# A kernel on one core with its whole instruction order written out: another order, and the last three accumulators copied whole

## The chip, the cores and the metric

The kernel runs on 1 core of one Trainium2 chip. Time is device microseconds (us) of one execution, the median of 3 runs. The engines are TensorE (PE; its weight loads are PEld), VectorE (DVE), ScalarE (ACT), GpSimd (POOL) and SyncE (SP, which issues most DMAs).

## What is computed

A recurrent attention with a complex decay, over 4 batches, 8 heads, 768 steps and head dimension 48; its output is the input of a feed-forward layer with a rational activation (384 -> 2048 -> 384, weights given in 8-byte floats).

```python
def _attn_ref(q, k, v, a_re, a_im):
    mag = np.sqrt(a_re * a_re + a_im * a_im)
    scale = np.minimum(mag, 0.999) / (mag + 1e-06)
    a_re_n, a_im_n = (a_re * scale, a_im * scale)
    ...
    for t in range(S):
        new_re = ar * S_re - ai * S_im
        new_im = ar * S_im + ai * S_re
        kv = np.einsum('bhd,bhe->bhde', k[:, :, t], v[:, :, t])
        S_re, S_im = (new_re + kv, new_im)
        y[:, :, t] = np.einsum('bhd,bhde->bhe', q[:, :, t], S_re)

def _moe_ref(x, w_in, w_out, a, b):
    h = x @ w_in
    h2 = h * h
    h3 = h2 * h
    P = a[0] + a[1] * h + a[2] * h2 + a[3] * h3
    Q = 1.0 + np.abs(b[0]) * np.abs(h) + np.abs(b[1]) * h2
    g = P / (Q + 1e-06)
    return (g @ w_out).astype(np.float32)
```

## The kernel before

The sequence is cut into 6 chunks of 128 steps; a chunk of one batch is a *unit*, so there are 24 units, taken in 12 pairs. For each unit the code records these steps:

- `norm` loads the decays (AA), squares and roots them, and makes the running product of their sizes MM (scans on DVE, three a unit) and the angle T. A small copy keeps the last column of MM in `ncar` for the next chunk.
- `angle` (once a pair) sums the angles, reduces them to one turn and makes the argument of the cosine, CO; `trig` takes arctangents, sines and cosines on ACT, which needs another activation table than the roots do.
- `outer` (line 569) loads QK and V, makes the factors RU out of MM, multiplies QK by RU, multiplies the result by CO and by T (two tiles Q) and has six DMAs copy the Q tiles into HQ, where a head's 96 rows lie on partitions.
- `attn` (line 599) transposes (PE, line 611), makes scores (line 624) with a mask ST, values (line 642) and the states for the next chunk (line 662), and writes the result into X, in two parts: rounded, and what is left.

The weights come in 8-byte floats: `weights` and `fold` (line 416) load 28 blocks (384 or 512 KB) into few staging buffers (`g` four, `wh0` to `wh2` one each) and put each block together in four steps, the last two on DVE (lines 443 to 449). `split` and `halve` (line 461) part them into a rounded and a left-over half. A buffer is loaded anew only when its block is done, so SP waits there.

The feed-forward `ffn` (line 678) runs eight times: twice on the first pair and second pair with whole fp32 weights, twice more on a pair each, then four times on two pairs with 512 columns. Each has 16 blocks: `first` (line 701) makes ph, ten or so operations of ACT, DVE and POOL (helpers at lines 351 and 366) make g, `reduce` (line 717) adds into the accumulators po. At its end po is scaled and copied (`evac`, line 380), and stored.

Nothing runs in the order in which it is recorded. `Plan` collects 2600 operations with what they read and write, and with the engines that each may run on; `recorded` (line 185) unpacks the string ORDER into a sequence of operation numbers, each with one of its allowed engines, checks that each stands behind all that it depends on, and the kernel emits them in that sequence. Each engine works its own operations off strictly in this order, and so do the queues of SP and of ACT, which also issues a few DMAs. An operation that waits holds up all behind it on its engine. `rouse` (line 667) records dummy matmuls, each of which may run on PE, or as nothing at all on SP: the order decides which. A product of two tiles in SBUF mostly may go to DVE or to POOL, a copy of kT or po to ACT or DVE, a weight step to two or three engines.

In the last feed-forward (`end`) each of the three accumulators po (512 columns) is copied in two halves, the first on ACT, the second on DVE, and stored by one DMA; that of the last one is issued by ACT.

Of the kernel before, what the change touches and what calls it, by code (L numbers as in the profile page):

```python
# [232 lines left out]


ORDER = (
    "c-lo+33yaR*1gq9x|2Xs6+jR&kO1Ni!=Q{fjsu8*D2OcMf`UP1SGJ%KWF0nvfb0VTf&x11_~U?pqJWBujx(dkfI^x@L`J9zOBO=+nNzQW|CjIe>wd55)~$Qb"
# [3 lines left out]
    "xW?Gfe`CcMEjQAOwT#bRyO5qm=!=T3l;6riEXS*%A9dsSPxdfcOJnmdn<BT#T1GXd{uPU(nzWQAW`R|*2Kn+cZVw%d`8@f*R}toCvcz<<%aoxFrX5werA11z"  # L240
    "a+ND)<d;fF_Tz@obU!1PvFFMuGLLa9kW~U)iVv4bXrNAH)^dsWD%Td>AY+M(kuFW{#SU8VE1ikgR!YKhJ~N|O$;J3oJ}cxkMh~;oq?sJTbg4>P5xEa_B#mP)"
    "W=`OKUzJDdzkO^y{=-;&jhjux%!rP|Khag5lnQ!30l+^PgZZ>IMF#3AwuV}v+v(}iJ@~hza`jT&i%qCWixrrGF?{w@J>?d<4X7>;nPk_CvEE5P71viBUxq@Q"
    "B=QREYVNgjPVVur6zY*KUC!V|J(u@abg3OhYgKqfI3txPPsFn~YRZhjQW=I~sr18H+%5;{`)XN@okZIh943-?Vt2ijQ6<Y|U;G0`Wil<L%AXjuKiSJzB6HA7"
    "R%s>Axl6?A2l0<(0%J3Umg5+UjrF7Gd~9R=?Xh;pmmp;Nx<Z^lk}Q-usz-dfjKWm$e$7QZ=TK1-&iV!qU@t4TuXyw%nRB)Y>trhZtiW@)L-OQhaD07LG#2~x"
    "9yb>QWU<aGt|P<a*U4GpZzSIXh4ghCF2Km7`h$;UnlWw^Hpo%j!1Z3xvt2&o7%b1o3VM@euA<l`oBDFh4#pw_46x)2`Ku|lRRlUks>svK@OnHg)0wxK(x2bI"
    ")s5Xl^nISL=`QFoc9cnxnl4G25KCt{`)}wb#~8!jSjk`C>e+UZ8SD-d0}(09JR>7q8LqNMx9E<}=V3Y8bI0f8CfW@1D(AbuqIZD$mvnaVFjSz22}!!k(GR#C"
    "dLn0ij8t>LUd46NtFlfyasTDmrH{y4tfO&yl6ze<uI>m<lG{$oOI-a5*=`{#IhEP{9=DSHK9ZS?!w51+4Aaa``!MUZg|6c6;h2}@3*2Q6;1TQNdPHt!6clSs"
    "$xQh>=8#i%>h><*OtpS}M_ehfD4^XK2FY&S!BvrII79qL$XrSW$p`%Wf>kt#JNyHYyN{JogLs+Bd?>lBBQB1%L_ux5OOHm&C5$oIv>wAmxz+S@{qPEkq#YUh"
    "0_#P|6S4)HiISGsCbyE4ydTwh^)<J+;rNAKl%N^My~t;!y!R)<l}yD;(lobO^ffFq1ME!x>MHlhIvry5t|F?Z$ZmAi<+2z>wxN^+R*%P(tY#FF$SbRvqmOVS"
    "pN_yBS)}{9+On5+KS6i-fxA|+3oG!p9KnRjn!8K7NCA3CQ~8t~C{;??2@cuDe3S3rn_;d3qmeDc$k8F$hBq1M#*!^b%mRq&&a@ViiTV|{iOh3`QR^u~^%z&3"  # L250
    "y8_CHbw#8+=$gs~c87ZOyepBr2zh+|XL(a^u)Cxy9+&s^9Ji6N&*xs75IOtMKIoU__zZVTy1d5yJ<LvbFINWkBC6NhJo>PLzON0ewd792%=HSS%V)YfpS0zE"
    "d+P06J4N2ZCFZj=;}?>5g8WRx5Shn3?9xZ=R*oKuq+mzN_`14XI`a1mtjy-}C9W})XT-DY#tr$c3tl8@Q{`^+5jNTW;;Xn5-ZlG)iYb`Pk&kl5JjuW_M#&p|"
    "njtFSx-9vQPcy{#?vd=v+st!zo$k$5YkGz;9b7JFe~jC>8_y0t54X4>{PcLvXAIxPA=(+n91mcXe$W215jQb1hxBOo6;A3#?2AdJhC74WoV^dehku7}CEYBw"
    "Q{l6Fk=e<TyXATI&k*-9US7vi6tRn!>)Q0B1pmP-lkRS3J~v@E{R)%qhA>La$RZDOMvg2)M_PJ^aoS-9;#SV;Cqs0hTga}t9vfvVa~)<y{lLz?nI4?yl`Grz"
    "Z=LUI>vWQ9z<ln(ol;ApdaHd_x|_jvKJ~!!_I_!>N>=h1?T5(iJJ>H2eN2{a^0aB^P9lfv#-s=F_Z(EvMY<7l?{m#v>{QP)mx~ZHL#*FR7UNlnU9_-+RdgEr"
    "(Od?ip&nJ-mrs}BGJLNb&Yl)xWJ1zjd}Y6dCmGY~?EFfeG4pM8uDyl(|Cl&^f{N&LkW0UIvJ|mDrStnAseqIW;oIf#8SiM;;4bdB8b_W(6FG=G`R->#;cLk2"
    "E6Y78Q_F$#_rUkix`CEc%wJ)ktt#*(t+yvL`lsXFDc+BxKe23NdcYk^ut!=^Rh*{PQ`9kgIJ%sbKy?;ix+UM;DF0*(LuBJ}oYHk!ufSa5RGGH!J)*7^*Zc!n"
    "t!i-_Uj+eD_ewo>lrQ=1G?LWCco#B9$kdbLI$Bi9s(YP2KSq@L9_c$}9acwGMsS<yWPz=$&9|AQwz5N>_BG2oc*rIyDMdW$vSpT}QxATDf8%;p4R@H@ZaZ3t"
    "S4vl~n%H}X{&hwjM&~T6<uYE!vqXFhUY(}V#uQZ17hJPI&9vscrOY__)TFsp`h*)pw#<;<Im#ERh#}P8laLhTc9?9ULQt+kKk5c!HnW?bsD7DFJy&Q;u!b{E"
# [853 lines left out]
```

## Time and profile before

| | us |
|---|---|
| median of 3 runs (607.23 to 609.35) | 608.46 |
| the profiled execution | 608.84 |
| its span, from first to last instruction | 607.1 |
| PE busy in the span | 558.8 (92%) |
| DVE busy | 545.7 (90%) |
| ACT busy, table loads included | 527.1 (87%) |
| POOL busy | 275.4 (45%) |

Over the whole span the DMA engines moved 64.02 MB; the first quarter carries most of it. Matmuls of one group overlap in the records, so a busy PE is not PE at its peak. A row of a timeline gives start and duration in us, engine, line, operation, what it writes and reads, how many instructions it merges and, in brackets, how long the engine stood idle before it and what ended that.

### The profile page before, as it was taken

Reading aid. Unit: us, or ns where it says so; the run is one execution under the profiler, and the core shown is the slowest. Engines: PE = TensorE matmul, PEld = TensorE weight load, DVE = VectorE, ACT = ScalarE, POOL = GpSimd, SP = SyncE. Lnnn points to the kernel's source line nnn. Section 1 sums busy time; section 2 is a strip of 40 time slices with the busy share of each in tenths; the row PEclk is TensorE's granted clock in tenths of the full one; section 3 lists DMA queues with packets and bytes.
Section 4 is the critical chain, followed back from the end, with each engine's and each line's share of the span. In section 5 each row is a group of like instructions: output and inputs, shape, how many; then the busy total and the mean of one; then the engine's idle time right before and its main releaser. Section 6 shows DMA issues by size and latency. Waiting matters only on the chain.

```text
span 607.1 us, 15647 instructions
## 1 busy us (share of the span) xinstructions
PE 558.8 (92%) x6236; PEld 468.3 (77%) x6236; DVE 545.7 (90%) x918; ACT 527.1 (87%) x870; POOL 275.4 (45%) x264
## 2 busy tenths in 40 slices
PE   3258989999999999998999999999999999999995
PEld 2246878778899999996888877888888888778884
DVE  6989979989999999999999999988899978779983
ACT  6978989989999999999999989988978787587871
POOL 4456455255655556624684544464726066200000
PEclk9669999999999999999999999999999999999998
DMA  8899436436551455537227147233464235010001
GB/s 268 282 253 285 148 79 152 111 57 149 110 136 41 89 128 127 129 103 154 51 64 157 35 106 168 74 60 82 75 102 127 26 73 103 3 52 2 1 1 58
DMA packets 39185, 64.02 MB, mean 105 GB/s; under 512 B 4416, under 2 KB 25152, under 8 KB 39104
## 3 DMA queue, kind: packets, MB, share of 16 engines
q1 hardware_dynamic: 38960, 62.67, 42.2%
q8 instruction: 51, 0.84, 0.6%
q14 instruction: 30, 0.25, 0.1%
q10 hardware_dynamic: 144, 0.26, 0.1%
HBM read 39.32 MB, written 4.72 MB: 73 GB/s over the span
## 4 chain that ended last, share of the span: by engine, by line
PE 47%; DVE 5%; ACT 3%; issue 1%; DMA 1%; DVEq 0%; ACTq 0%
PE po L717 20%; PE ph L701 20%; PE at L642 3%; PE at L624 2%; ACT Zf L366 1%; DVE Af L351 1%; PE at L662 1%; DVE Q L351 1%; DVE ph L351 1%; DMA AA<-in_aa 1%; PE at L611 1%; ACT Af L366 1%; DVE ST L351 0%; DVE g L351 0%; DVE MM L351 0%
## 5 line engine op out<-in xcount | busy, mean ns | idle before, releaser
L717 PE MATMUL po<-g,wh 128*128 128x512 f32 (+1 forms) x576 | 167.6, 360 | 0.0
L701 PE MATMUL ph<-X,wiH 128*128 128x512 f32 (+1 forms) x576 | 144.3, 363 | 2.2 <-DVE Af L351 2.2
L717 PE MATMUL po<-g,wo 128*128 128x256 f32 (+1 forms) x462 | 141.8, 370 | 0.1
L717 PEld LDWEIGHTS po<-g,wh 128*128 128x128 f32 x576 | 102.8, 189 | 18.2 <-issue 1.4
L701 PEld LDWEIGHTS ph<-X,wiH 128*128 128x128 f32 x576 | 97.3, 188 | 20.1 <-issue 1.4
L717 PEld LDWEIGHTS po<-g,wo 128*128 128x128 f32 x462 | 87.3, 191 | 12.5 <-DVE g L351 0.5
L351 POOL TENSOR_TENSOR g<-Af,Zf 128x512 fp32r<-128x512 f32 x30 | 40.2, 1341 | 115.7 <-ACT Zf L366 59.9
L351 DVE SCALAR_TENSOR_TENSOR ph<-Zf,co,ph 128x512 f32<-128x512 f32 x96 | 71.8, 748 | 8.9 <-ACT Zf L366 5.9
L366 ACT ACTIVATE Zf<-ph,co 128x512 f32<-128x512 f32 x96 | 65.3, 680 | 10.4 <-PE ph L701 5.6
L351 DVE SCALAR_TENSOR_TENSOR g<-ph,co,Zf 128x512 fp32r<-128x512 f32 x80 | 59.6, 745 | 14.7 <-ACT Zf L366 13.6
L366 ACT ACTIVATE Zf<-Af,co 128x512 f32<-128x512 f32 x80 | 57.8, 723 | 16.3 <-DVE ph L351 13.9
L366 ACT ACTIVATE Af<-Af,co 128x512 f32<-128x512 f32 x96 | 68.7, 720 | 0.8
L701 PE MATMUL ph<-X,wi 128*128 128x512 f32 (+1 forms) x264 | 67.4, 359 | 0.0
L351 DVE SCALAR_TENSOR_TENSOR Af<-Af,co,g 128x512 f32<-128x512 f32 x80 | 65.1, 814 | 2.2
L366 ACT ACTIVATE Af<-ph 128x512 f32<-128x512 f32 x96 | 56.2, 589 | 8.8 <-PE ph L701 8.6
L351 DVE SCALAR_TENSOR_TENSOR Af<-ph,co,Af 128x512 f32<-128x512 f32 x80 | 59.7, 746 | 1.4
L701 PEld LDWEIGHTS ph<-X,wi 128*128 128x128 f32 x264 | 45.7, 188 | 8.1
L366 ACT ACTIVATE Zf<-Zf 128x512 f32<-128x512 f32 x80 | 50.4, 630 | 1.8
L701 PE MATMUL ph<-wh,wi 128*128 128x256 f32 x192 | 45.9, 387 | 0.9 <-DVE g L351 0.9
L701 PEld LDWEIGHTS ph<-wh,wi 128*128 128x128 f32 x192 | 35.6, 190 | 7.1 <-issue 1.6
L351 POOL TENSOR_TENSOR SQ<-SQ 128x384 f32<-128x384 f32 x18 | 21.8, 1212 | 35.9 <-ACT SQ L366 35.8
L624 PEld LDWEIGHTS at<-HQ 96*32 96x32 f32 x1536 | 30.6, 113 | 9.7 <-ACT kT L357 3.7
(203 smaller groups left out, 1088.7 us busy)
## 6 DMA issues: line engine op xcount, KB each, us to landing
HQ<-Q SPq DMA_DIRECT2D x144, 128.0 KB, 5.0
AA<-in_aa SPq DMA_DIRECT2D x23, 384.0 KB, 4.1
QK<-in_qk SPq DMA_DIRECT2D x23, 384.0 KB, 4.2
V<-in_v SPq DMA_DIRECT2D x24, 320.0 KB, 5.3
wh<-in_w_in SPq DMA_DIRECT2D x6, 512.0 KB, 6.2
g<-in_w_out SPq DMA_DIRECT2D x8, 384.0 KB, 5.6
wh<-in_w_out SPq DMA_DIRECT2D x8, 384.0 KB, 6.4
g<-in_w_in SPq DMA_DIRECT2D x6, 512.0 KB, 6.6
```

The source lines that it names most:

```text
L351: call = lambda e: getattr(e, kind)(*map(real, args), **{k: real(x) for k, x in kw.items()})
L366: e.activation(o(), i(), f, **kw)
L611: e.transpose(pt[:, i].bitcast(F32R), hq[:, 4 * g + i, 1, :], ident)
L624: e.matmul(pst[32 * q:32 * q + 32, i + y, s0:C], hf[:, h, 1, s0:s0 + 32], hf[:, h, 0, s0:C], start=True, stop=True)
L642: e.matmul(py[32 * y:32 * y + 32, min(j, 2), :], l, sts[h // 4][:, h % 4, :] if q is None else hf[:, h, 0, :], start=q is None and j == 0, ...
L662: e.matmul(pd[m:m + 32, h], kT[:, h, m:m + 32], V[:, n:n + D], start=True, stop=True)
L701: e.matmul(o, wt[f // 4 * NJ + j][:, f % 4 * P:f % 4 * P + P], moving(j, hl), start=n == 0, stop=n == len(prods) - 1)
L717: e.matmul(o[:, cols], wt[:, j * P:j * P + P], gg, start=(f == 0 and n == 0 and cols.start == 0), stop=(f == NFF - 1 and n == len(prods) - ...
```

## The change

The string ORDER is replaced. As the new string unpacks, it holds 2597 operations: 863 on DVE (857 before), 792 on ACT (787), 235 on POOL (246), 420 on PE (418; 31 dummy matmuls instead of 29), 287 on SP (292). 179 of the operations that both orders have change their engine, and most change their place by some tens of operations, within the same course of units and feed-forwards. Six copies of accumulator halves become three copies of whole accumulators: in the new order DVE copies the last one, ACT the middle one, then DVE the first one.

```diff
 ORDER = (
-    "c-lo+33yaR*1gq9x|2Xs6+jR&kO1Ni!=Q{fjsu8*D2OcMf`UP1SGJ%KWF0nvfb0VTf&x11_~U?pqJWBujx(dkfI^x@L`J9zOBO=+nNzQW|CjIe>wd55)~$Qb"
...
+    "c-lQ!2Y8m%6@I@zJ0!U`EE#PQz)_{e5vUZEB?z(vg$gR5EKvhNnIXsq6Gen1j0izMhKwo%P-#I?P*jMvMW_`*0%5cW`EJ4pS^w#KZ>Z1z{Nww+JI;B}d){;I"
...
 )
@@ ffn @@
         for o, _, n, j in cuts:
             ob = buf(ff, [P, 512], F32, *(("Zf", ZB) if j == 0 else ("Af", AB) if F == 2 or j == 1 else ("wo15", 1)))
-            for h in range(2) if end else (0,):
-                m = n // (2 if end else 1)
-                cols = slice(h * m, h * m + m)
-                evac(m, lambda ob=ob, cols=cols: ob[:, cols], lambda o=o, cols=cols: o[:, cols], (o, "co"), ((ob, h),),
-                     minus if whole else sc, ("ACT", "DVE")[h:h + 1] if end else None)
+            evac(n, lambda ob=ob, n=n: ob[:, 0:n], lambda o=o, n=n: o[:, 0:n], (o, "co"), (ob,), minus if whole else sc)
```

## Rows read from the trace of the kernel before

**Rows 1.** Windows: stretch, length, busy us per engine, PEclk, DMA share, GB/s
```profile
0.00:60.00 60.00, 30.21 (x317) 23.32 (x318) 49.87 (x108) 48.22 (x90) 29.70 (x47) 0.80 0.91 274
60.00:100.00 40.00, 37.29 (x267) 30.83 (x265) 36.12 (x61) 36.50 (x61) 23.12 (x28) 0.96 0.48 122
100.00:360.00 260.00, 252.38 (x3526) 221.61 (x3526) 248.55 (x415) 245.21 (x404) 138.67 (x125) 1.00 0.45 103
360.00:600.00 240.00, 238.89 (x2131) 192.52 (x2129) 210.30 (x335) 196.38 (x316) 83.87 (x65) 1.00 0.29 62
90.00:100.00 10.00, 9.85 (x97) 7.75 (x95) 9.59 (x18) 9.00 (x17) 6.69 (x8) 0.83 0.60 135
```

**Rows 2.** The page, busy time of each engine over the span
```profile
PE 558.8 (92%) x6236; PEld 468.3 (77%) x6236; DVE 545.7 (90%) x918; ACT 527.1 (87%) x870; POOL 275.4 (45%) x264
```

**Rows 3.** Timeline, 0 to 61 us, single rows of DVE, ACT, POOL and PE
```profile
5.51 0.16 DVE L391 RECIPROCAL co<-ab 128x1 f32<-128x1 f32 x1 [1.85 <-DMA ab<-in_coef]
...
23.57 0.83 ACT L565 ACTIVATE T<-T 128x768 f32<-128x768 f32 x1
...
27.24 0.93 DVE L351 TENSOR_TENSOR Q<-QK,CO 128x768 f32<-128x768 f32 x1
...
38.59 0.57 DVE L443 SCALAR_TENSOR_TENSOR po<-po,wh 128x384 uint32<-128x384 uint32 x1 [2.89 <-ACT wh L439]
...
41.35 0.19 POOL L351 COPY ncar<-MM 128x3 f32<-128x3 f32 x1 [4.24 <-DVE MM L351]
...
50.41 0.86 PE L611 MATMUL at<-ident,HQ 128*128 128x128 f32 x8 [1.92 <-DMA HQ<-Q]
...
55.42 0.91 PE L701 MATMUL ph<-wh,wi 128*128 128x256 f32 x3
...
60.49 0.75 DVE L351 SCALAR_TENSOR_TENSOR ph<-Zf,co,ph 128x512 f32<-128x512 f32 x1
```

**Rows 4.** Groups by form: count, then busy us and mean ns, then idle before
```profile
L351 POOL TENSOR_TENSOR QK<-QK,RU 128x768 f32<-128x768 f32 x12 | 24.2, 2014 | 8.6 <-DVE RU L351 4.4 <-DMA HQ<-Q 3.4 <-DMA QK<-in_qk 0.4
L351 DVE TENSOR_TENSOR QK<-QK,RU 128x768 f32<-128x768 f32 x11 | 10.4, 949 | 1.8 <-DMA QK<-in_qk 1.8
L351 POOL TENSOR_TENSOR Z<-MM,Z 128x384 f32<-128x384 f32 x17 | 22.3, 1311 | 33.0 <-ACT Z L366 33.0
L351 DVE TENSOR_SCALAR Zf<-po,co 128x512 f32<-128x512 f32 x2 | 1.5, 751 | 0.3 <-PE po L717 0.3
```

**Rows 5.** Waits of SP's queue, 0 to 60 us: total us, times, longest
```profile
SPq L345 <- DVE wi L447: 12.7, 5, 5.6
```

**Rows 6.** Timeline, 79 to 96 us, single rows of SP, POOL and DVE
```profile
79.09 1.21 SPq L345 DMA_DIRECT2D HQ<-Q  x2
80.39 0.55 SPq L345 DMA_DIRECT2D QK<-in_qk  x1
...
87.61 1.80 POOL L351 TENSOR_TENSOR QK<-QK,RU 128x768 f32<-128x768 f32 x1 [3.40 <-DMA HQ<-Q]
...
90.41 0.56 DVE L351 SCALAR_TENSOR_TENSOR SQ<-AA,SQ 128x384 f32<-128x384 f32 x1 [3.29 <-POOL T L351]
...
92.96 0.95 DVE L351 TENSOR_TENSOR Q<-QK,T 128x768 f32<-128x768 f32 x1
...
93.19 2.46 POOL L351 TENSOR_TENSOR Z<-MM,Z 128x384 f32<-128x384 f32 x1 [2.81 <-ACT Z L366]
```

**Rows 7.** Timeline, 598 to 602 us, copies and the last store
```profile
598.78 0.47 ACT L357 ACTIVATE Zf<-po,co 128x256 f32<-128x256 f32 x1 [4.50 <-PE po L717]
...
599.29 0.48 DVE L351 TENSOR_SCALAR Zf<-po,co 128x256 f32<-128x256 f32 x1 [1.92 <-ACT Zf L357]
...
600.08 0.47 ACT L357 ACTIVATE wo<-po,co 128x256 f32<-128x256 f32 x1 [0.82 <-PE po L717]
...
601.49 0.33 SPq L345 DMA_DIRECT2D out<-Af  x1
```

**Rows 8.** Waits of PE for a DMA of HQ, whole span: total us, times, longest
```profile
PE at L611 <- DMA HQ<-Q: 4.7, 3, 2.0
```

More of the change, by code (lines that the diff above doesn't have):

```diff
@@ L240 @@
[L240 to L259, printed above, removed]
@@ new lines @@
+    "9|DiBYVi=}ens+KCJ~52D;$?7RPjkr?tzz7S>&Na0=lK~P?>nX=$bS~Ip1?IQM{zLi#<KjUyKZ?7KJl%kh4P2R|?QbT49<VV3HGe6rYfnxaK8EL}-#%9Eq_Q"
+    "$KPkUM@t;md;N^WGesVscsQlc`E4bDTDdA4^jrQW{9Rt)+!g46aKs}{M7E(VLXo7(%tdJ~ouJ@zrLV9{vgKLqmf`4)p0Y=K=0g>2Jl&h`J+f4J#g}Mt<KnCQ"
+    "+*;h19!JRy&WuKy&hR~2m78d7*o%*x_iJS&)+AbcqcD=ATObhw-Srr(N-QmU72U8~g<-RQT~6yI{wmH|ulM;OSSP>8bQskKy?swN)Ypiim$Z#*--kCO9Fue#"
+    "|1w8M;T41+PZqQcIsLuV!=pIXqOdSAFt2tSt=}o}E;bF&q~(c14*{&;oKQw=e#@T=o3#uU<<|Z;acprzER_oSlvjM1Yut;Gk`h=^8->OAPCmtd;+mGtm5GU-"
@@ new lines @@
+    "DfOGtipxa0yeJyYJYl3x2JiIBgC6Zj!WfB2$}OIYS>oxFeuZp8X)qh(xu?b`yyt8Q(B6USc5-1JVo@olgE8=QG_8#&s|rSYU8RH0Gy%t-8j)Z<FI9z`w>fgM"
+    "WFu30NgHpXq$tnS!!Wca4?aMIUhR*^yAq)z%nlV^7R8xiXe}p@Dxr+|e)%J#aYXv*Q1dDlsS-bnc4WyZ`3L#7m|l2zk?+!kgfk_<t+Z#HsUZ?oGG3-jQ!hh;"
+    "GKHvxVXX3yYrap|T|65F!TY>wGA)L-1)Oi8?sKTL)HCSc2%_Mb7Uc9+T$d4K_bPtdk;D0<Aimq_`h3<2tz<b8b(ERT$a<KM3Yj4b5P^C`E)z32V-fFlz%cSM"
+    "8Y|UFW=npsyXWDHglXn+V^^Gy6>6A?!GmP`&IGUc5Sn3~{??DgWNEHT`~><R&bNor9GxO-ouzMz;hnS6M~-1T21$u%Wb*#K`k#J|6v-PzDc5>|B0nfu%=T##"
@@ new lines @@
+    "jcf9j%lT?73tpym4RxOQwBj3NFxv6Dl4EM*Wx4LRK(Q>=P4HhoONyCwHR>6EGpbaC8IIK|O)W1@l~f&yMgBy6k113sX1N+?w#oza{+}{R#vw)r<u#L~ZZi=$"
+    "ubP<tI4!p$;4-fo8|69v-bOB5mPY!V^kkm?&eV!krAS64pBnHyHZTiU$qSsb9Ix=nbjiRb&J_8Us7{vua72OXVBWx)xLh+LX;e`%^W-(`<GNea5YrB;B~rKH"
+    "Zl{s&hce#NsaS=<+daF>Ec{kd$mzdIJ3g6-rgA5Brajhhr$fk>R2-7eBnErrgiOW9@*v*hh>!8O6iQPZK!2i~%*glDANn=KIGkR8t9qIFl7=N@?+Cm@_1eRy"
+    ")G)b%NNKBQ=&y>>AS%~yt-tVzzT7|)nZbCr!sECpE6C^<Y1=2#i&tODzZj({NWmicSUqJ@sTb?zOMEJS=gK=}J|o(LSFO;I<7RP2J&e-(%{cLc0djgQtio;M"
@@ new lines @@
+    "vxC@&<IMF3a8*5ImeH#h@U0$N>R}>U>j^}^y!0qF=tmhAH>xb4|Lxlx&PJXZZN8G_9B&b$CdvjX&H-LmOK-Gi1Rf@WB6C!sZ+TfO8?iu*GC?^m_hJhX@$heI"
+    "*>)L(9NK)G^M}&k1@b<#;&Iy8kR!TaxLR-iCEL|3vsZqLbJAV^<bR+-%}l&)by^27gFHQ^R+<j7lm6^*`55W;-YIt9r?}1r8Nkm^WFQW6_XhlIPcChcpH!yV"
+    "E{CW9XU!U7G>|&iidlM$kuO#8CIssluYuIMD^&hu-Olu8rnkf!da&P5D^o?($DkJiT70L1-0_AC<6bYxYK&2NCKi|F8zOR@PY!U`^)jA2AC$K-LAo#}j9TwU"
+    "vx@vAqwzV%RY*T-)n2Z)R3>npKTAHxUn8<z$i=7BZhG5Ct;NpZ=&}X2!pUV?dzH9f;Z-B%PMOmqYCk&aC;STHkj|X2+4l=}1atJ=)UhqnM*rwvlUQ8DpTt(@"
@@ new lines @@
+    "8fk<gx!@G~A@pJ-I-x+?;tMsMtZ0KDXiW(#$|rIj-Q{ko;Blfi*&GaZ^a5Zs^#b2kqN(^<Yy?`;l4V5wudbSQBZB4BkW-BQ@9_vTz7_B6lBRkIt$CU{5<x|J"
+    "(?4$`s9xrdsYquA1yD%*{~@)Kj5}DxAH!MI7|M)63&zpIX6Es2!Qp}Bao0_}!`Q=ko$cSGwyzSSV!67)FYbOrBJ`trn5=z(wiU>IP6^{#5kA*@SgltQ1^a42"
+    "-|nV$vFJg47{S=S;^*ki%*hZu%@~OD$i5ax3vZ<Ry^4CVoLX=vaZ15mRO7CAN{{z%kl6t;;&Up4Ma0wd%nx#tJQ#uynS<B4=Fd37T6RRNg<p%c^$A+hN&bcp"
+    "qyeq##XPOgxua><PppA^IHE5Zvr+ECAN6`h(Z;(6Ge&dNhmxkx`bBb>QFs<M11?E_KHn=Z;i}7wJeL(cIMyepzHkw50L!F4+V}_L8PrE6qaLBpQyGKo>cZ&r"
@@ L276 @@
+    "|5XT9)xH?`l%3Btvfv~m;1SsdE;H?!K9;E8v};m}?0+exQs;HFV`(Mhc!5>CPRqhwrM35M{PwaZ=9Q~a;Z9@f7-l`MWqw)q=v)5@R60NE5Dh_Ht+Ux$>6D~C"
+    "_pqyk5RXuYu-y93As!Y#+ojdsTHE#WJa5?OMYxfbWKfiirBgBMbp<;IYfH6=s@pZ}*EJ(yTy1;A|Bhpt{_1btu2oJg>voFZuWH9yPlua2EwkrtJKEO$m|O7)"
+    "zvY)jlPbYZAWR3zo>~=VYUF=QQFeI"
 )
```

35 lines of the change are left out of this document (16 added, 19 removed).

## The prediction

> **What bounds the kernel now.** I read the windows view first, in four stretches [rows 1]. From 0 to 60 us TensorE computes for 30.2 us only: the 16 DMA engines are 0.91 busy and VectorE 49.9 of 60 us. From 60 to 100 us TensorE works 37.3 of 40 us; from 100 to 360 us it works 252.4 of 260, with VectorE at 248.6 and ScalarE at 245.2, so three engines are nearly full at once; from 360 to 600 us TensorE works 238.9 of 240 us and sets the pace alone. The 7.1 us that are left to the span's end hold the last copies and stores. The page's line of busy time [rows 2] gives the same over the span: TensorE 92%, VectorE 90%, ScalarE 87%, GpSimd 45%.
>
> So no order can give much. What can be won is idle time of VectorE before about 360 us: from 0 to 60 us 10.1 us, of which 5.5 us come before its first work on loaded data [rows 3], so 4.6 us; from 60 to 100 us 3.9 us; from 100 to 360 us 11.4 us [rows 1]. After 360 us only an earlier start helps.
>
> **The change part by part.** I decoded both order strings against the kernel's recorded list and summed, for each engine, the mean durations of the rows grouped by form ([rows 4] has four of them) over all work queued ahead of one operation ("work ahead" below; rows overlap a little, so the sums stand some 7% above busy time).
>
> *What stays.* The order is valid as written: each operation comes once and behind what it depends on. The trips between trigonometric and root tables are 23 in both, so table loads don't change. Of 2591 common operations 179 change their engine; the total lists change by -3.4 us on VectorE, +1.9 us on ScalarE, +7.1 us on GpSimd. VectorE's list ahead of its first operation of the first feed-forward (at 60.49 us [rows 3]) is 53.2 us before and 52.8 after; ahead of the first feed-forward's fifth g 80.3 and 80.3; ahead of the first g of the sixth feed-forward 370.8 and 367.4. Bytes queued ahead of the last HQ copy of the first unit are 8.88 MB in both, of the second unit 11.88 MB in both. The gains have to come from waits inside the lists.
>
> *Front, to 60 us.* VectorE's longest wait there is 2.89 us at 38.59, for a weight block whose transfer came late [rows 3]. In the new order that step has 38.8 us of work ahead, not 30.4, so the blocks that are already there go first: the wait goes, and what is late next is the queue itself. GpSimd's 4.24 us wait at 41.35 [rows 3] goes too: it is a 3-column copy that stands ahead of the second unit's last Q product and waits for a scan with 32.7 us of VectorE work ahead; in the new order that scan has 24.0. So Q is whole some 4 us earlier, and its six DMAs, two of which ScalarE now issues, are no longer late against TensorE's 1.92 us wait at 50.41 [rows 3]. SP's queue is moved too: it waits 12.7 us for VectorE's weight folding [rows 5]; in the new order nine transfers go out before its first wait, not seven. Against this stands one new wait: the first unit's product with the sines goes from GpSimd to VectorE, and ScalarE gets four more operations, 2.6 us, ahead of the sine that starts at 23.57 [rows 3]. If ScalarE has no idle time it starts by 24.2, otherwise at 26.2, and ends 0.83 later; VectorE reaches the product with 20.6 us of work ahead, and before the change it was 21.0 us into its list at 27.24 [rows 3], so it arrives about 26.7: a wait between 0 and 0.4, and I take 0.4. Sum: 2.9 - 0.4 = 2.5 us, between 0 (the DMA engines decide) and 4.6 (all idle time goes).
>
> *60 to 100 us.* VectorE waits 3.29 us at 90.41 for GpSimd's T, which stands behind a product that waited 3.40 us for the fourth unit's QK transfer [rows 6]. SP issues that at 80.39, 1.30 us after the first HQ copy of the unit before, behind two copies [rows 6]; now one copy stands ahead, which saves 0.6 us. The third unit's product, 0.95 us on VectorE, goes to GpSimd at 2.01 [rows 4], as does one more Q product, which leaves VectorE 1.9 us lighter there. I take 1.0 us of 3.3, ends 0 and 3.3. The clock fell here once, to 0.83 in the mean of 90 to 100 us [rows 1], between its levels of 2.4 and 1.2 GHz, after TensorE had been waiting; 3.4 us at the lower level cost at most 1.7 us, counted only for the range.
>
> *100 to 360 us.* VectorE's list is 3.4 us lighter by the sixth feed-forward, but ScalarE is as full as VectorE [rows 1] and its list there is only 2.1 us lighter. I take 1.2 us, ends -3.4 and +3.4: the trace can't show which waits a new order makes, and their likeliest size is that of the ones they replace.
>
> *Dummy matmuls.* 31 run instead of 29, in time when TensorE waits: nothing; if that cover is gone, under 1 us.
>
> *Tail.* Three accumulators were each copied half by ScalarE, half by VectorE, and the halves ran one behind the other (598.78, then 599.29; the VectorE half waited for ScalarE's) [rows 7]. Now VectorE copies the last accumulator whole, then the first; ScalarE copies the middle one. A whole copy takes 0.75 us on VectorE [rows 4]. The last matmul released the last accumulator's copy at 600.08 [rows 7]; two copies behind each other end at 600.08 + 0.75 + 0.75 = 601.58, and SP issues the last store then, against 601.49 [rows 7]: 0.1 us lost, ends -0.5 and +0.7.
>
> Sum: 2.5 + 1.0 + 1.2 - 0.1 = 4.6 us. From the span of 607.1 us that leaves 602.5; 1.74 us lie around the span (608.84), and that execution stands 0.38 above the median 608.46: 603.9 us.
>
> **The rivals.**
> - *Transfers set the front, and nothing is carried on.* For: the DMA engines are 0.91 busy up to 60 us [rows 1], with equal bytes ahead of both units, equal lists on VectorE. Against: VectorE and SP stand waiting for each other there [rows 3, 5]. Then the front gives 0, the middle up to 1, the tail -0.1: 607.1 + 0.1 + 1.36 = 608.6 down to 607.6, no difference; I put it at 607.9.
> - *Longer chains on GpSimd (slower).* The product QK of a unit is on GpSimd in 17 units instead of 12, at 2.01 us instead of 0.95 [rows 4], and it stands in the chain product, Q, HQ copy, transposes and scores. Five units, 1.06 us each, are 5.3 us, if in each the HQ copy is what TensorE waits for last; it decides from the point where the copy lands later than the feed-forward work queued beside it runs out. Against: GpSimd is 45% busy [rows 2], and TensorE waited for that copy 3 times, 4.7 us in all [rows 8]. With the front's 2.5 gained and no more: 607.1 + 5.3 - 2.5 + 1.74 - 0.38 = 611.3.
> - *VectorE loses to GpSimd what it hands over.* A GpSimd multiply of 384 columns took 2.46 us at 93.19, beside two VectorE products of 0.95 each, against 1.31 in the mean [rows 4, 6]. So far GpSimd pays, not VectorE. If VectorE paid for the 7.1 us that GpSimd's list grows, half of it would take back 3.6 of the 4.6 us: 607.5. The Trainium skill ("SBUF — State Buffer", Who interferes with whom) says that a VectorE instruction with two SBUF inputs contends with a GpSimd instruction that reads SBUF, and that the later one to issue blocks whole. By that rule VectorE would pay wherever GpSimd issues first; the trace shows GpSimd paying.
> - *The string is not taken* and the kernel plans its own order: its length and its dependencies fit, so 0.01.
>
> **How the numbers follow.** Forecast 0.50 (own range 599.5 to 606.4), front bound by transfers 0.22, GpSimd chains 0.20, VectorE pays 0.05, others 0.03. All the terms at their upper ends and the clock come to 4.6 + 2.1 + 2.3 + 2.2 + 0.6 + 1.7 = 13.5 us; they will hardly meet, so the lower end takes some 6 us beyond the forecast: 598.0. The upper end takes in the slower rival: 611.4. A measurement of this kernel can tell about 0.3%, 1.8 us, from no change: faster 0.52, same 0.25, slower 0.23.
>
> **What would show it.** Right: no VectorE wait near 38 us, the first feed-forward's matmuls before 53.5 us instead of 55.42 and VectorE's first operation on them near 58 instead of 60.49; the wait for T under 90 us short of 2.5 us; the last store issued 1.5 us behind the start of the last accumulator's copy. Wrong: TensorE's first transposes of the second unit not before 50 us (transfers), or waits of TensorE for HQ copies in units whose product moved to GpSimd (slower).

## The result

The changed kernel takes 601.15 us (median of 4 runs, 599.88 to 602.38), the kernel before 608.9 beside it (607.23 to 610.21): ratio 0.9874, 95% interval 0.9838 to 0.9911. It is faster by 1.3%, 7.7 us; the forecast was 603.9 us, 4.6 us below the median then known. Its profiled execution took 602.15 us, with a span of 600.5; that of before had 607.1.

The windows of the changed kernel (as [rows 1]):

```profile
0.00:60.00 60.00, 29.27 (x306) 22.74 (x307) 50.12 (x107) 46.89 (x88) 31.04 (x46) 0.77 0.87 266
60.00:100.00 40.00, 40.00 (x364) 34.76 (x363) 38.92 (x74) 39.72 (x69) 24.13 (x25) 1.00 0.58 140
100.00:360.00 260.00, 256.36 (x3475) 225.65 (x3474) 249.05 (x418) 246.04 (x408) 149.29 (x127) 1.00 0.46 106
360.00:600.00 240.00, 232.68 (x2101) 187.03 (x2099) 205.57 (x328) 192.09 (x311) 79.86 (x56) 0.99 0.26 62
90.00:100.00 10.00, 10.00 (x177) 8.53 (x176) 10.00 (x21) 9.94 (x19) 6.98 (x9) 1.00 0.71 139
```

Read TensorE first, the first figure with a count. From 60 to 100 us it worked 37.29 us and now works all 40.00; from 100 to 360 us it worked 252.38 and now 256.36 [rows 1]. Its idle time in these two stretches fell from 10.33 to 3.64 us, by 6.7 us, and the span fell by 6.6. These figures count dummy matmuls as work: in the first feed-forward eleven of them run now and eight before, and where ten are moved away (below) 3.45 us of idle time come back there and that stretch gets no longer. Up to 60 us TensorE works less than before, at a lower clock. The page's line of busy time has hardly moved [rows 2], since the work is the same:

```profile
PE 558.3 (93%) x6240; PEld 470.2 (78%) x6240; DVE 543.7 (91%) x924; ACT 524.7 (87%) x872; POOL 284.3 (47%) x253
```

The front, single rows of the timeline (as [rows 3]):

```profile
24.61 0.96 DVE L351 TENSOR_TENSOR Q<-QK,CO 128x768 f32<-128x768 f32 x1 [0.41 <-ACT Q L357]
...
48.34 1.23 PE L611 MATMUL at<-ident,HQ 128*128 128x128 f32 x8 [4.43 <-DMA g<-in_w_out]
...
51.91 0.69 DVE L351 TENSOR_TENSOR ST<-at,cmask 128x512 f32<-128x512 f32 x1 [4.70 <-ACT ph L431]
...
56.70 2.75 PE L701 MATMUL ph<-wh,wi 128*128 128x256 f32 x12
...
61.05 0.75 DVE L351 SCALAR_TENSOR_TENSOR ph<-Zf,co,ph 128x512 f32<-128x512 f32 x1
```

VectorE's wait of 2.89 us at 38.59 and GpSimd's of 4.24 at 41.35 [rows 3] are gone, and the one new wait that I priced at 0.4 us is there with 0.41. But the first feed-forward's matmuls start at 56.70 us, not before 53.5 as I wrote; before it was 55.42. The second unit's transposes come 2.07 us earlier (48.34 against 50.41 [rows 3]), and from there to the first feed-forward 8.36 us pass instead of 5.01. The windows say why (stretch, length, TensorE's busy time, granted clock, DMA share, GB/s; 0.50 is the level of 1.2 GHz, 1.00 that of 2.4):

```profile
44.00:46.00 2.00, 0.00 (x0) 1.00 1.02 223
46.00:48.00 2.00, 0.00 (x0) 0.59 1.03 369
48.00:50.00 2.00, 1.66 (x10) 0.50 1.01 372
54.00:56.00 2.00, 2.00 (x33) 0.50 0.00 0
56.00:58.00 2.00, 2.00 (x8) 0.85 0.36 48
```

TensorE had come to the upper level shortly before (0.76 in the mean of 42 to 44 us) and then stood idle from 43.9 to 48.3 us; the level fell, and the whole second unit was computed at half speed. Before the change TensorE was at 1.00 in each 2 us from 48 to 56, though it had stood idle there too, for 1.92 us [rows 3].

From 60 to 100 us, rows of GpSimd, SP and VectorE (as [rows 6]):

```profile
75.98 1.81 POOL L351 TENSOR_TENSOR Q<-QK,T 128x768 f32<-128x768 f32 x1
...
77.82 0.33 SPq L345 DMA_DIRECT2D QK<-in_qk  x1
78.20 3.17 SPq L345 DMA_DIRECT2D HQ<-Q  x5
...
84.21 1.82 POOL L351 TENSOR_TENSOR QK<-QK,RU 128x768 f32<-128x768 f32 x1
...
87.44 0.55 DVE L351 SCALAR_TENSOR_TENSOR SQ<-AA,SQ 128x384 f32<-128x384 f32 x1
```

The fourth unit's QK load goes out at 77.82, not 80.39; GpSimd's product does not wait (3.40 us before), VectorE's step behind T does not wait (3.29 us before [rows 6]). The label of the 3.40 us names an HQ copy, but it was the QK load: that landed at 87.47 us, and the product started at 87.61. The tail (as [rows 7]):

```profile
592.52 0.69 ACT L357 ACTIVATE Af<-po,co 128x512 f32<-128x512 f32 x1 [4.87 <-PE po L717]
...
593.20 0.75 DVE L351 TENSOR_SCALAR wo<-po,co 128x512 f32<-128x512 f32 x1 [2.40 <-PE po L717]
...
593.86 0.74 DVE L351 TENSOR_SCALAR Zf<-po,co 128x512 f32<-128x512 f32 x1
...
594.63 0.33 SPq L345 DMA_DIRECT2D out<-Zf  x1
```

The last store is issued 1.43 us behind the start of the last accumulator's copy, against 1.41 before [rows 7].

### The profile page after: what moved, and what is told of

It is laid out like the page before. It is cut to its first block, busy times and chain, and to the rows that moved or that the text cites. A ratio compares the mean times of both kernels' runs of the same rounds, so it can differ in the third digit from the quotient of the medians.

```text
span 600.5 us, 15652 instructions
## 1 busy us (share of the span) xinstructions
PE 558.3 (93%) x6240; PEld 470.2 (78%) x6240; DVE 543.7 (91%) x924; ACT 524.7 (87%) x872; POOL 284.3 (47%) x253
## 4 chain that ended last, share of the span: by engine, by line
PE 46%; ACT 11%; DVE 8%; issue 2%; DMA 1%; SPq 0%; DVEq 0%; ACTq 0%
PE ph L701 20%; PE po L717 19%; ACT Zf L366 4%; PE at L642 4%; PE at L624 2%; DVE Af L351 2%; ACT Af L366 2%; DVE g L351 2%; DVE ph L351 2%; PE at L662 1%; ACT L366 1%; ACT SQ L366 1%; DMA QK<-in_qk 1%; DVE Q L351 1%; PE at L611 1%
## 5 line engine op out<-in xcount | busy, mean ns | idle before, releaser
L717 PE MATMUL po<-g,wo 128*128 128x256 f32 (+1 forms) x462 | 140.3, 367 | 0.0
L351 POOL TENSOR_TENSOR RU<-MM,RU 128x384 f32<-128x384 f32 x18 | 22.7, 1259 | 39.4 <-DVE RU L351 33.4
L351 DVE TENSOR_TENSOR ST<-at,cmask 128x512 f32<-128x512 f32 x48 | 31.6, 683 | 10.1 <-ACT ph L431 4.7
```

The source lines that it names most:

```text
L351: call = lambda e: getattr(e, kind)(*map(real, args), **{k: real(x) for k, x in kw.items()})
L717: e.matmul(o[:, cols], wt[:, j * P:j * P + P], gg, start=(f == 0 and n == 0 and cols.start == 0), stop=(f == NFF - 1 and n == len(prods) - ...
```

## The experiments

In the table, "ratio" is against the kernel before on the same chip, with its 95% interval. The other columns come from the one profiled execution of each kernel: the start of the first feed-forward's first matmul; from there to the end of its last (A); from there to the end of the last matmul of the fifth feed-forward (B); from there to that of the eighth (C). Span less these is the tail, 6.9 to 7.6 us in all of them.

| kernel | ratio | first matmul, us | A | B | C |
|---|---|---|---|---|---|
| before | 1 | 55.42 | 58.95 | 252.07 | 233.61 |
| changed | 0.9874 (0.9838 to 0.9911) | 56.70 | 53.57 | 249.15 | 233.74 |
| changed, again | 0.9880 (0.9844 to 0.9917) | 52.49 | 54.65 | 248.59 | 233.74 |
| new front, old rest | 1.0019 (0.9998 to 1.0040) | 53.65 | 59.49 | 249.58 | 234.29 |
| old front, new rest | 0.9914 (0.9881 to 0.9946) | 54.04 | 54.75 | 248.38 | 233.72 |
| new to 103 us, old rest | 1.0008 (0.9978 to 1.0038) | 56.15 | 59.96 | 250.66 | 234.00 |
| new to 219 us, old rest | 0.9913 (0.9886 to 0.9940) | 54.22 | 53.67 | 250.28 | 234.27 |
| old to 220 us, new rest | 0.9981 (0.9953 to 1.0009) | 55.14 | 58.30 | 249.83 | 233.74 |
| before, own QK buffer | 0.9977 (0.9948 to 1.0006) | 55.23 | 55.89 | 251.32 | 233.87 |
| before, early third unit | 0.9938 (0.9907 to 0.9968) | 54.31 | 57.41 | 252.76 | 233.57 |
| changed, late QK load | 0.9882 (0.9848 to 0.9916) | 54.23 | 54.94 | 249.04 | 234.58 |
| changed, QK on VectorE | 0.9837 (0.9803 to 0.9871) | 52.94 | 54.44 | 252.35 | 232.74 |
| changed, dummies moved | 0.9861 (0.9825 to 0.9898) | 52.70 | 53.65 | 248.60 | 233.74 |
| and waits filled | 0.9832 (0.9804 to 0.9859) | 53.23 | 53.41 | 249.08 | 233.72 |

Executions of one kernel differ: 26 of the kernel before on one chip lie between 604.38 and 611.95 us. The first column shows where much of that comes from: 52.49 and 56.70 us in two executions of the same changed kernel, whose spans differ by 3.8 us. A and B repeat better, so I read stages from them and whole times from the ratios.

### Which stretch gains: two pairs of exchanged orders

My theory, from the two traces: the new front gives nothing, all gain is made behind it. The rival is my prediction: the front gives 2.5 us. An order is a list; a first part of one and, of the other, all that is not in it make a valid order. Here and below, most fences with + and - tell in words which part of an order, or which steps of an engine's queue, moved.

```diff
# new front, old rest: against the order of before
-old[0:263]
+new[0:244]
 old, what is left
# old front, new rest: against the changed order
-new[0:244]
+old[0:263]
 new, what is left
```

> The new order up to the first matmul of the first feed-forward (its first 244 operations), then the old order for all that is left; the last accumulators copied whole. My theory, read from the two traces: the new front gives nothing (first feed-forward matmul at 56.70 us against 55.42 before), because TensorE runs at the lower clock level from 46.5 to 57 us; all of the gain is made behind it. Then this kernel takes what the old one takes, 608 to 610 us, and VectorE's wait of about 3 us for T near 90 us is still there. Rival: the new front is worth 2.5 us as I predicted, and the first feed-forward's late start is made up by work done ahead: 605.5 to 606.5 us.

> The reverse of the run before it: the old order up to the first matmul of the first feed-forward (its first 263 operations), then the new order for all that is left; the last accumulators copied whole. My theory (the new front costs 1.3 us and the rest gains): first feed-forward matmul at 55.4 us, whole time 599 to 602 us, as good as the changed kernel or up to 1.3 us better. Rival (the front's 2.5 us are real and are carried on): 603 to 604.5 us, some 2.5 us worse than the changed kernel.

Measured: 609.44 us for the new front with the old rest, 602.74 for the old front with the new rest, the kernel before 608.0 beside them. The first matches my theory: the front alone brings nothing. Three rows show what it ran into:

```profile
79.09 0.54 SPq L345 DMA_DIRECT2D QK<-in_qk  x1
...
87.90 0.50 PE L611 MATMUL at<-ident,HQ 128*128 128x128 f32 x4 [2.01 <-DMA HQ<-Q]
...
89.18 0.56 DVE L351 SCALAR_TENSOR_TENSOR SQ<-AA,SQ 128x384 f32<-128x384 f32 x1 [3.37 <-POOL T L351]
```

Both waits of the old order are there in full. A is 59.49 us although the clock is at 1.00 all through 60 to 100 us in this trace: the waits alone cost the time, the fall of the clock to 0.83 [rows 1] is no condition for it. The old order up to 220 us (below) does not show that fall either, and its A is 58.30. The second, 5.3 us faster, lies just above my theory's 599 to 602 and just below the rival's 603 to 604.5: with the new rest behind it, the front may be worth up to some 2 us, and the intervals of 0.9914 and of the changed kernel overlap.

The same with later seams:

```diff
# new to 103 us
+new[0:500]
 old, what is left
# new to 219 us
+new[0:1082]
 old, what is left
# old to 220 us
+old[0:1088]
 new, what is left
```

> The new order for its first 500 operations (to about 103 us, the third unit's and the fourth unit's products with it), then the old order for all that is left; the last accumulators copied whole. The trace of the changed kernel is 4.7 us ahead at the end of the first feed-forward's last first-layer matmul, 2.5 us ahead at 270 us and 7.0 us ahead at 366 us. My theory (two separate gains, the first made between 60 and 100 us and kept, the second made behind 100 us by the new order there): 603 to 605 us. Rival A (the first gain decides everything, and the rest of the old order simply runs on from it): 600.5 to 602.5 us. Rival B (the first gain is given back in the old order's waits): 606 to 608 us.

Measured: 609.18 us, no gain. The waits of its TensorE from 88 to 125 us (total us, times, longest):

```profile
PE at L623 <- ACT kT L356: 4.7, 1, 4.7
```

The lead of the first feed-forward was lost in this one wait at 105.7 us, at the seam, where operations that the old order had done earlier piled up on GpSimd; ScalarE, which copies kT, waited 3.14 us for GpSimd's MM. Behind the wait the clock fell once more, to 0.83 in the mean of 110 to 120 us. The run says nothing of the old order behind it. So the next seams lie where the two lists have done nearly the same.

> The new order for its first 1082 operations (to about 219 us, a place where the two orders have done nearly the same), then the old order for all that is left; the last accumulators copied whole. The run with the seam at 103 us lost its lead in one TensorE wait of 4.7 us at the seam, so it told nothing of the stretch behind. My theory (two gains: about 4.7 us made by 220 us, and about 2 us more made behind it, in the stretch from 270 to 366 us): this kernel keeps the first alone: 602.5 to 605 us, profiled span near 602. Rival (the order behind 220 us does not matter, the old one has the same waits): as good as the changed kernel, 600 to 602 us. Rival (the lead is given back in the old order's later waits): 606 to 608 us.

> The reverse: the old order up to about 220 us (its first 1088 operations), then the new order for all that is left; the last accumulators copied whole. My theory: only the second gain is left: 605 to 606.5 us, and in the trace the last matmul of the third and the fourth feed-forward stands where the old order had it (220.7 and 272.3 us), that of the fifth some 2 to 4 us ahead of the old order's 366.4 us. Rival (all gain comes from the stretch up to 220 us): 607.5 to 609 us.

Measured: 602.63 and 605.84 us beside 608.24; the changed kernel, run with them, 600.44. Differences of 5.6 and 2.4 us, together 8.0, against 7.8 for the whole order. So there are two gains, as the theory said. The smaller one alone does not stand clear of no change by its ratio, but the traces place it: column B is 250.28 with the old order behind 219 us and 249.83 with the new one from 220 us, and the part of B from the third feed-forward's last matmul on is 143.5 to 143.7 us in each of the seven traces that have the new order unedited there, 144.6 to 147.4 in the six that have the old. What makes this second gain can be read from the two first traces: in that part TensorE stands idle for 4.9 us before and 2.7 after, and the part is 145.8 and 143.5 us long. Gone are 1.6 us for the thirteenth unit's HQ copies (a row below), 0.9 for VectorE's masked scores ST, 0.5 for X and 0.2 for kT; waits for the feed-forward's Af grew by 0.9. With the old order behind 219 us it is idle for 4.5 us, with the new one from 220 us for 2.6.

### What cost the time between 60 and 100 us

Theory A: the fourth unit's QK load, late, holds GpSimd's T and so VectorE (3.29 us [rows 6]). Theory B: the third unit's HQ copies, which go out 3 us earlier in the new order, are as important. First the load alone, in the kernel before:

```diff
     def spot(shape, name, c, bb):
-        pool_, ring, *n = ALT[name] if (c, bb) == (0, 1) else (wk, name)
+        pool_, ring, *n = ALT[name] if (c, bb) == (0, 1) else (cst, "wh4") if (c, bb, name) == (0, 3, "QK") else (wk, name)
# SP's queue: QK of the fourth unit from behind two HQ copies to ahead of them all
```

> The kernel before, whole, with one thing changed: the fourth unit's QK has a buffer of its own (one that is free from 35 to 106 us), so that its load need not wait until the third unit's Q products have read the only QK buffer, and SP issues it at about 71.5 us instead of 80.39. Theory A (VectorE's wait of 3.29 us at 90.41 us for T is what costs; it stands behind that load): the wait is gone, TensorE's fall to the lower clock at 90 us too, and the time falls by 3 to 5 us, to 603.5 to 605.5 us. Theory B (TensorE's wait of 2.0 us for the third unit's HQ copies, issued 3 us later in the old order than in the new, costs as much by itself): the wait for T is gone, but TensorE still waits some 2 us near 88 us and falls to the lower clock, and the time falls by 1 to 2 us, to 606.5 to 607.5 us.

```profile
71.54 0.43 SPq L345 DMA_DIRECT2D wh<-in_qk  x1
...
87.84 0.51 PE L611 MATMUL at<-ident,HQ 128*128 128x128 f32 x4 [0.64 <-DMA HQ<-Q]
```

The load went out at 71.54 us and VectorE's wait for T was gone. TensorE's wait for the HQ copies fell too, to 0.64 us, though the first was issued as late as before (79.08 us). With no load between them the last went out 1.5 us earlier and landed at 87.39 us, not 88.81; so this edit moved the copies as well, and does not part the two theories cleanly. A fell by 3.1 us in the trace, whose execution (605.12 us) is the second fastest of ten, but the times fell by 0.23% only, with an interval that reaches zero. That is closer to theory B's 1 to 2 us than to A's 3 to 5, while B's own signs, a wait of 2 us and the fall of the clock, did not come.

Then the reverse, the load alone made late in the changed kernel:

```diff
 SP:  HQ(third unit, 1st)
-     QK(fourth unit)
      HQ(third unit, 2nd to 6th)
+     QK(fourth unit)
```

> The changed kernel with one transfer moved back: the fourth unit's QK load stands on SP's queue behind the last of the third unit's HQ copies instead of behind the first, so it is issued at about 81.4 us of the first trace instead of 77.8 (80.39 before the change). All other queues are the changed kernel's. Theory A (the time of that load made the gain between 60 and 100 us): GpSimd waits for it, VectorE waits 2 to 3.5 us for T as before the change, TensorE runs dry behind it, and the time rises by 3 to 5 us, to 603.5 to 605.5 us. Theory B (the gain there is mainly the third unit's HQ copies, 3 us earlier, which this run leaves where they are): VectorE's wait comes back, TensorE's idle time and the time rise by 1 us or less.

```profile
78.84 0.59 SPq L345 DMA_DIRECT2D QK<-in_qk  x1
...
83.89 1.83 POOL L351 TENSOR_TENSOR QK<-QK,RU 128x768 f32<-128x768 f32 x1 [1.82 <-DMA QK<-in_qk]
...
86.72 0.56 DVE L351 SCALAR_TENSOR_TENSOR SQ<-AA,SQ 128x384 f32<-128x384 f32 x1 [1.33 <-POOL T L351]
```

VectorE's wait came back with 1.33 us, and the ratio stayed at 0.9882. Theory A's 3 to 5 us did not come: A is 54.94 us, 0.3 to 1.4 above the unedited kernel's two traces. The place of that load on SP's queue, the very thing that I had costed, is worth little here, some 1 us by A; the intervals bound it only at some 3 us.

What set both transfers was the step ahead of them. A row of the kernel before:

```profile
79.40 0.95 DVE L351 TENSOR_TENSOR Q<-QK,CO 128x768 f32<-128x768 f32 x1
```

It ends at 80.35, and the QK load was issued at 80.39 [rows 6]: units share one QK buffer, and the load waited until the third unit's last Q product had read it. SP itself was busy with the two HQ copies ahead until 80.30 [rows 6], so the queue and the buffer held the load almost equally long, and neither alone could have let it go earlier; both hang on the third unit's Q products. In the new order the last of these ends at 77.79 us and the load goes out at 77.82, while SP stands waiting for it. So, in the kernel before, the third unit's chain moved, and with it one step of the fourth unit (its RU, ahead of two weight steps on VectorE):

```diff
 ScalarE:  cosine and sine of the third unit's angles
-  behind two steps of the first feed-forward's fourth activation
+  one and two steps earlier
 VectorE:  Q with the cosines    -at 79.40   +behind the weight fold at 75.17
           RU, fourth unit       -behind two weight folds   +ahead of them
 GpSimd:   Q with the sines      -behind two weight folds   +ahead of them
 SP:       -HQ 4th, 6th, QK(fourth unit), HQ 5th, 2nd, 1st, 3rd
           +HQ 3rd, 2nd, 1st, QK(fourth unit), HQ 4th, 6th, 5th
```

> The kernel before, whole, with one chain moved: the third unit's cosine and sine stand one and two steps earlier on ScalarE's queue, its two Q products earlier on VectorE's and GpSimd's, so that the second ends near 78 us instead of 80.34, and its six HQ copies and the fourth unit's QK load go out from about 76.5 to 81 us instead of 79.09 to 84.37 (76.04 to 81.37 in the changed kernel). Theory (this alone makes most of the gain between 60 and 100 us: the transfers are then through before the 16 KB of program code that a queue loads near 81 to 82.7 us, behind which the old kernel's QK load took 7.08 us): the QK load lands within 5 us of its issue, VectorE's wait for T falls from 3.29 us to under 1, TensorE's for the HQ copies from 2.0 us to under 0.5, the first feed-forward's last first-layer matmul ends 3 to 5 us earlier than at 98.02, and the time falls by 2 to 4.5 us, to 604 to 606.5 us. Rival (the gain there needs the rest of the new order too, its feed-forward steps in another sequence): the waits shrink and others take their place, the time falls by less than 1 us.

```profile
78.94 0.33 SPq L345 DMA_DIRECT2D QK<-in_qk  x1
...
84.32 1.82 POOL L351 TENSOR_TENSOR QK<-QK,RU 128x768 f32<-128x768 f32 x1 [0.17 <-DMA QK<-in_qk]
```

Measured: 605.71 us beside 609.34, ratio 0.9938: 3.6 us, within the theory's 2 to 4.5. VectorE's wait for T and TensorE's for the HQ copies are both gone. The trace also bears the rival out in part: TensorE now waited 2.0 us in all for the first feed-forward's g and 1.5 for kT between 60 and 115 us, and A fell by 1.5 us only. The load landed 5.24 us behind its issue, not within 5, and the last first-layer matmul came 2.6 us earlier, not 3 to 5. So this chain makes a good part of the first gain: by the whole times 3.6 of the 5.6 us made up to 219 us, by column A 1.5 of 4.8; the two readings differ, and no run says which is nearer. The rest lies in the feed-forward's steps or in more of the new sequence; no run separated it further.

### The front and TensorE's clock

> The changed kernel itself once more, beside the next three on the same chip, for a second trace of it and a time that the three can be compared with. My theory, that its first feed-forward starts late because TensorE runs at the lower clock level while the second unit is worked on (46.5 to 57 us in the first trace), expects the same again: first feed-forward matmul between 55.5 and 57 us, time 600 to 602.5 us. The rival, that this was an accident of one execution: full clock at 50 us in this trace, first feed-forward matmul near 53.5 us.

The changed kernel once more, unedited: 600.44 us. Windows and rows of this second trace:

```profile
46.00:48.00 2.00, 1.91 (x18) 0.74 0.89 314
48.00:50.00 2.00, 2.00 (x64) 0.50 0.98 350
50.00:52.00 2.00, 2.00 (x41) 0.91 0.61 243
```

```profile
46.09 0.84 PE L611 MATMUL at<-ident,HQ 128*128 128x128 f32 x8 [2.16 <-DMA HQ<-Q]
...
52.49 2.86 PE L701 MATMUL ph<-wh,wi 128*128 128x256 f32 x12
```

Here TensorE stood idle for 2.16 us, not 4.43; the clock fell all the same, but was back by 52 us, and the first feed-forward started at 52.49. The fall is no accident of one execution, its length is: in each of the seven traces with the new front unedited, TensorE works at 0.50 for some or all of the second unit. The length of the idle time alone doesn't tell when: the new front has 1.70 to 4.43 us of it ahead of the second unit's transposes, the old front 0.45 to 2.39 us and in none of five traces a fall behind it. What decides is not shown. In seven traces that have the new front unedited the first matmul stands between 52.49 and 56.70 us, 54.3 in the mean; in five with the old front between 54.04 and 55.42, 54.8 in the mean.

Now ten dummy matmuls that stood among the first feed-forward's matmuls go into that idle time:

```diff
 PE:  values, first unit; dummy
+     10 dummies
      transposes, scores, values, second unit; first feed-forward
-     10 dummies, among its first eight matmul groups
```

> The changed kernel with ten of its dummy matmuls moved: they stood between 59 and 73 us, among the first feed-forward's matmuls, and now stand directly ahead of the second unit's transposes, in TensorE's idle time from 43.9 to 48.3 us; nothing else moves. Theory A (TensorE's clock in the front costs): the granted clock stays at its upper level to 60 us, the second unit's transposes to the first feed-forward matmul take 5.0 us as before the change, not 8.4, that matmul comes at 53 to 54 us, VectorE's wait of 4.7 us for the scores falls to about 2.7, and the time falls by 1.5 to 3 us against the changed kernel. Theory B (VectorE's list sets the front): the matmul comes earlier, VectorE's first operation of the first feed-forward stays near 61 us, and the time stays within 0.5 us of the changed kernel.

```profile
46.00:48.00 2.00, 2.00 (x14) 1.00 0.87 267
50.00:52.00 2.00, 2.00 (x49) 1.00 0.62 245
```

```profile
47.45 0.99 PE L611 MATMUL at<-ident,HQ 128*128 128x128 f32 x8
...
52.70 5.45 PE L701 MATMUL ph<-wh,wi 128*128 128x256 f32 x24
```

The clock stayed at 1.00 from 44 to 60 us, transposes to first matmul took 5.25 us, VectorE's wait for the scores was 2.77. In the seven traces without this edit the step from transposes to first matmul took 6.4 to 8.5 us, so the dummies in the idle time do keep the clock up. The matmul came at 52.70 us, a little ahead of theory A's 53 to 54, but no earlier than in the trace of the unedited kernel beside it (52.49, with 6.40 us). The time was 599.37 us, 1.1 below that kernel, less than theory A's 1.5 to 3, and the intervals of the two overlap: the gain in time is not shown. Last, VectorE's and ScalarE's waits there are filled with work that was ready:

```diff
 VectorE:  +2 scans and 1 product of the fourth unit
            scores x mask, second unit (2)
           -2 scans and 1 product of the fourth unit
 ScalarE:  +2 weight halvings
            kT copies, second unit (2)
           -2 weight halvings
```

> The kernel with the ten dummy matmuls ahead of the second unit's transposes, and with five more steps moved: on VectorE two scans and one product of the fourth unit (1.5 us in all, ready by 47 us) go ahead of the second unit's two masked copies of the scores, for which VectorE waited 2.78 us; on ScalarE two weight halvings (1.1 us) go ahead of the copy of the second unit's transposes, for which it waited 2.1 us. Theory (VectorE's list sets the first feed-forward, and what is done in a wait is won): the wait shrinks to about 1.3 us, VectorE's first operation of the first feed-forward comes 1 to 1.5 us earlier, and the time falls by 0.5 to 1.5 us against the run with the dummies alone (599.4): 598 to 599 us. Rival (TensorE is full behind 60 us and takes up nothing of it): no difference, 599 to 600 us.

```profile
50.41 1.29 DVE L351 TENSOR_TENSOR ST<-at,cmask 128x512 f32<-128x512 f32 x2 [0.65 <-PE at L624]
...
61.26 0.75 DVE L351 SCALAR_TENSOR_TENSOR Af<-Af,co,po 128x512 f32<-128x512 f32 x1 [1.04 <-ACT po L366]
...
64.58 2.83 PE L701 MATMUL ph<-wh,wi 128*128 128x256 f32 x12 [2.51 <-DVE g L351]
```

VectorE's wait shrank from 2.77 to 0.65 us, and its first operation of the first feed-forward came 9.5 us behind the transposes, not 10.6. Then it waited 1.04 us for ScalarE's po, for which it had not waited with the dummies alone: what was won in one wait was lost in the next. The rival's outcome came, no clear difference (599.18 us on another chip, intervals that overlap), but its reason did not: TensorE is not full there. It waits 2.51 us for g where the dummies had stood, and 2.44 us at the same place in the run with the dummies alone. The ratio of 0.9832 is the lowest of all, but its interval overlaps those of the changed kernel and of the runs near it.

### Are longer GpSimd chains dear?

```diff
 QK product of units 3, 8, 13, 19, 23:
-  GpSimd
+  VectorE
```

> The changed kernel with the product QK of five units (third, eighth, thirteenth, nineteenth, twenty-third), which the new order had moved from VectorE to GpSimd, back on VectorE at the same place of the list; 0.95 us each there, 2.01 us on GpSimd. My rival of longer GpSimd chains expects the time to fall by 2 to 5 us, since each chain gets 1.06 us shorter. My theory now (TensorE waits for no HQ copy behind 60 us in the changed kernel's trace, so the chains have slack and VectorE's time is the dearer one): the time rises by 0.5 to 4 us, 601 to 604.5 us, most of it from the third unit, where VectorE is full and the QK buffer comes free later.

Measured: 600.37 us, ratio 0.9837 (0.9803 to 0.9871), which overlaps the changed kernel's intervals: the whole times don't settle it, and my 0.5 to 4 us of loss are not confirmed by them. Stage by stage, in one trace, the move back costs 3.2 to 3.8 us in B and gains 1.0 in C. A row of this kernel with a window of its clock, and a row of the kernel before:

```profile
276.47 1.20 PE L701 MATMUL ph<-X,wiH 128*128 128x512 f32 x3 [1.65 <-DVE Af L351]
```

```profile
278.00:280.00 2.00, 2.00 (x6) 0.50 1.16 135
```

```profile
279.11 0.85 PE L611 MATMUL at<-ident,HQ 128*128 128x128 f32 x8 [1.58 <-DVE QK L351]
```

With QK on VectorE, TensorE waits 1.65 us for VectorE's feed-forward step, which the product has pushed back; in the changed kernel the longest such wait near there is 1.15 us. Behind the longer wait the clock fell, to 0.85 in the mean of 270 to 280 us and to 0.98 in that of the next 10. That is 3.4 us at the lower level and costs at most 1.7 us (an estimate from these means), so up to half of the loss in B is the clock's, in one execution. In the old order TensorE waited at this place for the thirteenth unit's HQ copies (the label names their product; the last of them landed at 278.87).

## Why the prediction was right, and where its steps failed

The time lay in the range, 2.8 us below the forecast, and the side was right. The terms of the sum were not: the front was put 2.0 us too high in the mean of the traces, the stretch from 60 to 100 us 3.8 us too low, the next one 1.3 too low. That the sum came this near is in part luck.

- *Front, 2.5 us forecast.* VectorE's and GpSimd's waits went as written, and Q was whole earlier: the last HQ copy of the second unit was issued 5.6 us earlier. The gain reaches the second unit's transposes: they start at 46.95 us in the mean of the seven traces with the new front, at 49.61 in that of the five with the old, 2.7 us earlier. It was not all that the copies had won. In the first trace the four that SP issued landed a median of 7.2 us behind their issue and ScalarE's two 7.8, where the six had taken 5.7, and TensorE's wait for them did not go, as I had written, but was 1.70 to 4.43 us long. So a part of the first rival, full DMA engines, was right. Then came a term that I didn't have: the clock fell behind that wait, and from the transposes to the first feed-forward 7.4 us pass in the mean, not 5.2. My text weighed the clock only at 90 us. Of the 2.7 us, 0.5 are left at the first feed-forward's first matmul, less than its scatter.
- *60 to 100 us, 1.0 us forecast, 5.0 at most with the clock.* This is the mis-sized term: A is 58.95, 59.49 and 58.30 us with the old order, 53.57 to 54.75 with the new, some 4.8 us. The failed step is "now one copy stands ahead, which saves 0.6 us". I took SP's queue alone for what held the QK load. The buffer held it as long, free 0.04 us before the issue, and both went with the third unit's Q products, 2.6 us earlier now. And I costed one wait, VectorE's, while TensorE's 2.0 us for the same unit's HQ copies [rows 8] hung on the same product.
- *100 to 360 us, 1.2 us forecast.* Column B gives some 2.5 us in the mean (249.58 to 252.76 where all of it has the old order, 248.38 to 249.15 where it has the new), inside the bounds of 3.4. That the next waits would be as long as those they replace was too careful, most of all for the thirteenth unit's HQ copies, 1.6 us.
- *Dummies 0, tail 0.1 lost.* The tail is as forecast. The dummies' places matter for the clock: ten of them moved kept it up.
- *Longer GpSimd chains (slower).* In the changed kernel TensorE waits for no HQ copy behind 60 us, so no chain decides, and with QK back on VectorE the time did not fall by the 2 to 5 us that this rival asked for.
- *VectorE loses to GpSimd what it hands over.* I gave this 0.05, since the row at 93.19 us [rows 6] showed GpSimd paying. There VectorE's product had started first, at 92.96. In the changed kernel a row shows the reverse:

```profile
184.52 1.83 POOL L351 TENSOR_TENSOR Q<-QK,T 128x768 f32<-128x768 f32 x1 [1.76 <-DVE QK L351]
```

```profile
184.53 2.64 DVE L351 TENSOR_TENSOR Q<-QK,CO 128x768 f32<-128x768 f32 x1
```

VectorE's product of 768 columns, 0.95 us elsewhere [rows 6], took 2.64 where GpSimd's had started 0.01 us ahead: 1.69 us lost, nearly GpSimd's whole 1.83. The Trainium skill ("SBUF — State Buffer", Who interferes with whom) says that the later one to issue blocks whole; this row agrees. Nor was it new: in the kernel before a VectorE step that takes 0.75 us elsewhere took 2.35.

```profile
340.44 1.85 POOL L351 TENSOR_TENSOR QK<-QK,RU 128x768 f32<-128x768 f32 x1
```

```profile
340.49 2.35 DVE L351 SCALAR_TENSOR_TENSOR Af<-Af,co,g 128x512 f32<-128x512 f32 x1
```

As an estimate over the two traces, take the VectorE steps that overlap one of GpSimd's and last over 0.25 us longer than the lower quartile of their operation and shape: they lose 8.2 us in 12 places before, 11.1 us in 14 in the changed kernel. So VectorE did pay, by some 3 us more than before, close to the 3.6 us of this rival, and the time fell all the same. The mechanism is real, but it did not decide the time.

## What to carry to other kernels

When a load is late, look for the instruction that ended just before its issue: a queue position alone holds it only if nothing else released it at that moment. A step that is done earlier may leave TensorE idle at the wrong place, so read the granted clock along with every wait that you move, and put dummy matmuls into the idle time, not behind it (here that held the clock up; 1.1 us of time, not clear of the scatter). Judge an order by exchanging parts at places where both orders have done the same, and take stage lengths from several traces, since one execution's front can differ by 4 us from the next.
